# Convolution taps of two channels per TensorE product, flat tables, and masks as seven products, in an S4 + MLP kernel

## The chip, the core and the metric

The kernel runs on one core of a Trainium2 chip. The core has five instruction streams that meet only at semaphores: TensorE (PE, with its weight loads shown apart as PEld), VectorE (DVE), ScalarE (ACT), GpSimd (POOL) and SyncE (SP), which here only issues DMAs. Each stream executes its instructions in the order in which the program lists them. The metric is the device time of one execution in microseconds (us); lower is better.

## The reference, cut to what matters

One sequence of 2048 positions with 512 channels goes through a state-space convolution (S4) and an MLP, each with a residual.

```python
dt = exp(log_dt)[:, None];  logdA = dt * (A_re + 1j*A_im);  dB = dt * (B_re + 1j*B_im)
l = arange(L).astype(bfloat16)                        # positions, rounded to bf16
P = exp(logdA[:, :, None] * l)                        # 512 x 128 x 2048
K = einsum("dn,dnl,dn->dl", C, P, dB).real            # 512 channels x 2048 taps
y = causal_convolution(K, layernorm(x)) + layernorm(x) * Dskip       # by FFT of length 4096
h = x + y
out = h + (gelu(layernorm(layernorm(h)) @ w1 + b1) @ w2 + b2)        # 512 -> 1376 -> 512
```

Since `l` is rounded to bf16, the taps K[d, l] are needed only at positions of the form a + 8b. The exponential of a sum is a product of exponentials, so K at a + 8b is, per channel d, the real part of a sum over the 128 states n of A[n, a] * B[n, b]: a small matrix product with n as the contracted dimension.

## The kernel before, in words

The 128 partitions of the big tables hold the 128 states n. Channels are split into four chunks of 128 (`CW`), c = 0..3, and the chunks into two pairs, q = 0 (c = 0, 1) and q = 1 (c = 2, 3). The program is one recorded list of operations. `Sched.add` records each with its engines, a planned cost and its dependences; the list `ORDER` (L166), found beforehand by a search and written out as numbers, fixes the order in which they are emitted, and with it the order on each engine (a negative number takes the second engine that an operation allows). `Sched.run` goes through `ORDER` once with a planned time, only to choose PSUM slots and to put in filler products (`fill`, L1378), and emits. A flag `hv` marks operations that the planner holds to lock DVE and POOL against each other.

Stages, with the lines of the profile:

1. **Setup.** Small inputs are loaded and transposed (L712, L746). `th` holds dt * A_re (L726, L571, sign turned at L559). `bexps` (L732) writes the magnitudes of the table B by 16 exponentials of 1024 columns; `aexps` (L941, L945, L949, L952) writes those of the table A. BatchNorm statistics of x are L871. POOL makes constants.
2. **Chains** (`chain`, L960). The phases of the tables are gathered in PSUM by products with small weights (L986), read out by ACT as sines and cosines into the buffers `SC` (L988, two of 1024 columns for each group of 4 rows, three buffers in turn), and multiplied into the magnitudes by DVE: B, for each half of the channels four groups of a sine and a cosine product on both sides of a centre row and one change of sign (L1007, L1008, L1006), and A, five groups with two products each (L1007 and L1008 for the first half, L993 and L994 for the second). The centre rows of B are set by POOL (L1313, L1314, L1337, L1338). In this stage POOL also makes the masked weights `W`, 7 x 4 small products of `valW` with a column of `msk` (L561 under `PTS`; the order gives 24 to POOL and 4 to DVE), and `BD` (L1329) and `DD`.
3. **Taps.** For q = 0, `kgen` (L1015) makes for each channel two products (real and imaginary) with 20 columns of A as weights and 33 columns of B as data (L1030, L1031), four channels at a time side by side in four column tiles of 32; both tables hold channels innermost, so neighbouring elements of a product's weights and of its data lie 256 bytes apart. For q = 1, `kgen4` (L1046) makes two products for four channels together, with 128 columns as weights (4 channels x 32 rows, 20 of them used, the pad rows zeroed by L1301 and by a DMA of 768 KB) and 132 columns as data (L1061, L1062); of the 4 x 4 blocks of the result the diagonal is used. Results go from PSUM to `Kg` by `evac` (L513 when ACT takes it, L515 when DVE does).
4. **Spectra.** `kspec` (L1095) maps taps to a first DFT stage with `W`, `kstage` turns the result through DRAM (`AK_d`) and `fstage` (L912) does the second DFT stage. `xspec` (L893, L912) does the same to the input, from `unorm` (L881).
5. **Inverse** (L1135 on DVE, L1145 on PE, turned by transposing DMAs L1151), `tail` (L1214 and following) and the MLP (`mlp`, L1268 to L1292).

```python
o = pst(p)[32 * g:32 * g + NA, 512 * nb:512 * nb + NB * n].rearrange("p (k i) -> p k i", i=n)[:, :, i]
pe.matmul(o, lhsT=Ar.ap()[:, :, d], rhs=Br.ap()[:, :, d], start=True, stop=False, tile_position=(0, 32 * g))
pe.matmul(o, lhsT=Ai.ap()[:, :, d], rhs=Bi.ap()[:, :, d], start=False, stop=True, tile_position=(0, 32 * g))
```

Of the kernel before, what the change touches and what calls it, by code (L numbers as in the profile page):

```python
# [15 lines left out]
P = 128  # L16
# [11 lines left out]
NB = 33  # L28
# [122 lines left out]
class VS(V):  # L151
# [93 lines left out]
class Sched:  # L245
# [42 lines left out]
    def run(self, nslots):  # L288
# [13 lines left out]
        for code in ORDER:  # L302
# [16 lines left out]
            if e == "POOL" and o.hv:  # L319
                for a, b in hold:  # L320
                    if a <= s < b:
                        s, end = b, b + c
# [62 lines left out]
def kernel(ctx, tc, A_u, A_A_re, A_A_im, A_B_re, A_B_im, A_C_re, A_C_im, A_log_dt, A_Dskip,  # L385
# [53 lines left out]
    Dz = take(bf16, NCH, 32)  # L439
# [34 lines left out]
    Kg = [take(bf16, NB, 2, 32), at(sc0 - 512, bf16, NB, 4, 2, 32)]  # L474
    zlo = take(bf16, NB, 2, 32).lo
    AK0 = take(bf16, 16, 2 * CW).lo
    XB = [at(lo + 16384, bf16, 8, 512) for lo in (E0, BA0)]
    PR = [[at(rest0 + 2048 * n, bf16, 8, CW) for n in range(4)], [take(bf16, 8, CW) for _ in range(2)] + [at(lo + 24576, bf16, 8, CW) for lo in (E0, BA0)]]
    Z = [[at(lo, bf16, P, 16) for lo in q] for q in ((zlo, sc0 + 8192), (EA2.lo + 11264, IA2.lo + 11264))]
    assert pos[0] <= NBYTES, pos[0]  # L480
    EA = [at(E0 + c * ASZ, bf16, NA, CW) for c in range(2)]
    EB = [at(EB0 + c * BSZ, bf16, NB, CW) for c in range(NCH)]
    IA = [at(BA0 + c * ASZ, bf16, NA, CW) for c in range(2)]
    IB = [at(IB0 + c * BSZ, bf16, NB, CW) for c in range(NCH)]
    ALL = slice(None)
# [46 lines left out]
    class Tmp:  # L532
# [3 lines left out]
        def __call__(self, dt, *shape):  # L536
# [883 lines left out]
```

## Time and profile before

| | us |
|---|---|
| median of 3 runs (lowest, highest) | 264.26 (263.89, 266.27) |
| the profiled execution | 262.47 |
| its span, first to last instruction | 260.1 |
| busy in the span: PE / DVE / ACT / POOL | 230.3 / 183.3 / 176.8 / 61.8 |
| setup, up to the first product of the chains on DVE | 47.45 |
| chains, to the end of the last of them on DVE | 47.45 to 90.6 |
| taps of q = 1, spectra, start of inverse and MLP | 90.7 to 165 |
| MLP with the rest of the inverse | 165 to 256.5 |

How to read it: a row of a timeline gives start and duration in us, engine, line, operation, what is written from what with its size, how many instructions were merged, and in brackets what the engine waited for. A row of the groups gives the busy time in us, the mean duration of one in ns, and idle time just before. Durations of neighbouring instructions overlap on one engine (they are pipelined), so what an instruction costs in a stream is the distance from start to start. PE busy counts such overlapping records and says little of how full PE is. The granted TensorE clock was 0.999 of full speed over the span.

### The profile page before, as it was taken

To read this page: it belongs to the slowest core of one execution; us is meant where nothing else is said; L and a number is where in the kernel's file an instruction comes from. 1 tells how busy PE (TensorE), PEld (TensorE's weight loads), DVE (VectorE), ACT (ScalarE), POOL (GpSimd) and SP (SyncE) were. 2 spreads that over 40 slices of the span, in tenths; PEclk is the share of its full clock that TensorE was granted. 3 is DMA by queue.
4 is the path that set the end of the run, shared out by engine and by line. 5 is a ranking of instruction groups with operands and counts; after the bars stand their busy time and mean duration, and the time that the engine had idled before them with its cause. 6 is when DMAs were issued, how large, how long until landed. Compare 5 with 4: busy or idle time off the path is not lost.

```text
span 260.1 us, 7656 instructions
## 1 busy us (share of the span) xinstructions
PE 230.3 (89%) x3236; PEld 133.7 (51%) x3249; DVE 183.3 (70%) x368; ACT 176.8 (68%) x214; POOL 61.8 (24%) x234
## 2 busy tenths in 40 slices
PE   7215997888997999989999998899999999999994
PEld 3102673454876586444467765555553434444452
DVE  3999997999999964679899778974615676222021
ACT  2679989999977977578989956966514701762700
POOL 9930871699996000000000000000000000000000
PEclk9999999999999999999999999999999999999999
DMA  6940012000001247729835985560771040214202
GB/s 161 211 108 2 4 38 28 3 4 3 3 5 57 72 164 222 249 93 283 279 112 88 143 161 176 97 170 3 117 131 36 0 93 20 61 28 96 69 15 66
DMA packets 40371, 23.88 MB, mean 92 GB/s; under 512 B 25649, under 2 KB 37778, under 8 KB 40338
## 3 DMA queue, kind: packets, MB, share of 16 engines
q1 hardware_dynamic: 39746, 22.95, 36.8%
q10 hardware_dynamic: 592, 0.46, 0.8%
q8 instruction: 25, 0.41, 0.6%
q14 instruction: 8, 0.07, 0.1%
HBM read 10.03 MB, written 6.29 MB: 63 GB/s over the span
## 4 chain that ended last, share of the span: by engine, by line
PE 57%; DVE 25%; ACT 11%; issue 5%; POOL 0%; DVEq 0%; ACTq 0%; POOLq 0%
PE ps L1268 15%; PE ps L1290 15%; PE ps L1145 8%; PE ps L893 5%; ACT ar L988 4%; ACT ar L513 4%; DVE ar L871 4%; PE ps L912 4%; DVE ar L1007 3%; DVE ar L576 3%; DVE ar L571 2%; PE ps L1095 2%; PE ps L1061 2%; DVE ar L1008 2%; DVE ar L559 2%
## 5 line engine op out<-in xcount | busy, mean ns | idle before, releaser
L513 ACT CAST ar<-ps 128x1024 bf16<-128x1024 f32 (+3 forms) x72 | 65.2, 970 | 19.3 <-PE ps L1145 6.9
L1270 ACT ACTIVATE ar<-ps,ar 128x512 bf16<-128x512 f32 (+1 forms) x44 | 28.2, 686 | 36.7 <-PE ps L1268 36.6
L561 POOL TENSOR_SCALAR ar<-ar 128x128 bf16<-128x128 bf16 (+6 forms) x44 | 39.6, 921 | 7.6 <-ACT ar L583 7.3
L1290 PE MATMUL ps<-ar 128*128 128x512 bf16 (+3 forms) x180 | 39.1, 367 | 0.4
L1268 PE MATMUL ps<-ar 128*128 128x512 bf16 (+1 forms) x176 | 39.3, 379 | 0.0
L515 DVE CAST ar<-ps 128x1024 bf16<-128x1024 f32 (+2 forms) x28 | 30.6, 1113 | 11.9 <-ACT ar L513 4.0
L988 ACT ACTIVATE ar<-ps 128x1024 bf16<-128x1024 int16 x36 | 35.1, 1032 | 5.1 <-DVE ar L1007 1.6
L1135 DVE TENSOR_TENSOR ar<-ar 128x1024 bf16<-128x1024 bf16 x48 | 30.7, 687 | 10.3 <-PE ps L1145 9.9
L1292 DVE TENSOR_TENSOR ar<-ps,ar 128x512 bf16<-128x512 f32 (+1 forms) x17 | 11.1, 660 | 37.7 <-PE ps L1290 35.0
L1290 PEld LDWEIGHTS <-ar 128*128 128x128 bf16 (+1 forms) x187 | 17.9, 98 | 20.0 <-issue 0.8
L1268 PEld LDWEIGHTS <-ar 128*128 128x128 bf16 (+1 forms) x176 | 17.3, 100 | 20.5 <-issue 0.8
L986 PE MATMUL ps<-ar 128*32 128x256 f16 x560 | 21.4, 275 | 5.0 <-ACT ar L988 3.1
L1145 PEld LDWEIGHTS <-ar 64*128 64x128 bf16 x768 | 21.6, 94 | 5.4 <-issue 3.0
L1145 PE MATMUL ps<-ar 64*128 64x128 bf16 x768 | 23.9, 217 | 0.3 <-ACT ar L513 0.3
L986 PEld LDWEIGHTS <-ar 128*32 128x32 f16 x560 | 14.3, 97 | 12.5 <-issue 12.2
L912 PE MATMUL ps<-ar 128*64 128x512 bf16 (+1 forms) x160 | 17.7, 342 | 1.2 <-DMA ar<-AK_d 0.6
L732 ACT ACTIVATE ar<-ar 128x1024 bf16<-128x1024 f32 x16 | 15.6, 1041 | 3.2 <-DVE ar L559 3.2
L893 PE MATMUL ps<-ar 128*32 128x512 bf16 x256 | 16.0, 381 | 0.3 <-ACT ar L513 0.3
L576 DVE SCALAR_TENSOR_TENSOR ar<-ar 128x4 f32<-128x4 f32 (+5 forms) x44 | 14.2, 327 | 2.5 <-ACT ar L583 1.4
L583 ACT ACTIVATE ar<-ar 128x512 f32<-128x512 f32 (+8 forms) x18 | 11.9, 681 | 4.9 <-DMA ar<-in_A_log_dt_dram 1.8
L1008 DVE TENSOR_TENSOR ar<-ar 128x1024 bf16<-128x1024 bf16 x21 | 14.6, 719 | 0.0
L1007 DVE TENSOR_TENSOR ar<-ar 128x1024 bf16<-128x1024 bf16 x21 | 14.5, 716 | 0.1
(99 smaller groups left out, 318.6 us busy)
## 6 DMA issues: line engine op xcount, KB each, us to landing
ar<-AK_d SPq DMA_DIRECT2D x8, 512.0 KB, 5.6
ar<-in_A_u_dram SPq DMA_DIRECT2D x4, 512.0 KB, 9.2
AK_d<-ar SPq DMA_DIRECT2D x2, 1024.0 KB, 4.6
AK_d<-ar SPq DMA_DIRECT2D x4, 512.0 KB, 4.0
out_dram<-ar SPq DMA_DIRECT2D x30, 64.0 KB, 2.0
ar<-in_B_w_dram SPq DMA_DIRECT2D x4, 344.0 KB, 6.0
ar<-in_B_w_dram SPq DMA_DIRECT2D x2, 640.0 KB, 6.6
ar<-ar SPq DMA_DIRECT2D x1, 768.0 KB, 5.4
```

Of the source, the lines that this page charges most:

```text
L513: act.copy(out_fn(), in_fn())
L515: dve.tensor_copy(out_fn(), in_fn())
L561: en.tensor_scalar(a, b, f(s1), f(s2), op0, op1)
L893: pe.matmul(pst(p)[32 * cg:32 * cg + 32, 512 * z:512 * z + 512], lhsT=BD.ap()[:, 32 * f + 2 - 2 * jl:32 * f + 34 - 2 * jl], rhs=un[2 * (2 ...
L912: pe.matmul(pst(p)[64 * h:64 * h + 64, w * (k + r):w * (k + r) + w], lhsT=T.ap()[:, f, r, :], rhs=v[f:f + 1].ap()[:, 0, :], start=True, st ...
L986: pe.matmul(pst(p)[32 * g:32 * g + 32, 256 * j:256 * j + 256], lhsT=W2[DELTAS.index(d)].ap(), rhs=S2[g].ap()[:, ch0:ch0 + 256], start=Fals ...
L988: add("ACT", c_act(1024), lambda e, p=p, sc=sc, cs=cs: act.activation(swo(sc[cs]) if hf and kind == "B" else sc[cs].ap().rearrange("p a b ...
L1135: dve.tensor_tensor(o, a, b_[:, :, ::-1, :] if sw else b_, ALU.mult)
L1145: pe.matmul(pst(p)[:, 512 * h + 128 * k:512 * h + 128 * k + 128], lhsT=q.ap()[rows, 2 * k + r, :], rhs=TP[w].ap()[rows, f0 // 2 + k, :], s ...
L1268: pe.matmul(pst(p)[:fs, 512 * z:512 * z + 512], lhsT=w1s[dc].ap()[:, fc * P:fc * P + fs], rhs=ybuf.ap().rearrange("p (t c) k -> p c t k", ...
L1270: add("ACT", c_act(512, 1), lambda e, p=p, z=z, fc=fc, fs=fs: act.activation(hT.ap()[:fs, fc, :], pst(p)[:fs, 512 * z:512 * z + 512], ACT. ...
L1290: pe.matmul(pst(p)[:, 512 * z + c0:512 * z + c1], lhsT=hT.ap()[:fs, fc, 128 * t:128 * t + 128], rhs=w2s[fc].ap()[:fs, c0:c1], start=(fc == ...
```

## The change

It does the following; numbers of lines are those of the kernel before unless said otherwise.

- One `kgen(q)` takes the place of `kgen` and `kgen4`. For each of the 64 channel places d of a pair's half, and for two such halves s side by side in two column tiles of 64, a product has 52 columns of A as weights: 20 rows of one chunk, 12 rows of zeros, 20 rows of the other chunk of the pair, 64 bytes from element to element. Its data are 72 columns of B: 2 chunks x 9 groups x 4 neighbouring rows, in runs of 4 elements. Of the 2 x 2 blocks (chunk by chunk) the diagonal is used. Each pair has 256 products (before: 512 for q = 0, 128 for q = 1) and 5 evacuations of 1008 or 864 columns (before: 4 of 726 or 330 columns for q = 0, 12 of 792 or 264 for q = 1).
- A lies as 4 x 52 x 32 per pair, B as 9 groups x 1024 (128 channel places x 2 chunks x 4 rows) per pair. All of `EB`, `IB`, and both pairs of `EA`, `IA` are laid out this way; the four gaps of zeros are filled by four memsets (`gap`), which takes the place of L1301 and of the DMA of 768 KB. The centre of B is a group of its own.
- The DVE products of the B chains take 1024 elements in one run, those of the A chains 2 x 4 runs of 128. ACT does the reordering when it writes sines and cosines (L988) and magnitudes.
- `Kg` has 37 instead of 33 rows, one of them a copy; `kspec` reads runs of 64 instead of 32 channels.
- The 28 small mask products become 7 of 512 elements each, `valW` times an expanded mask `mskx` (one copy of 896 elements). The order gives all of these to POOL.
- `th` is made by two products of 256 columns (before: two of 256 and two of 128) and turned in sign by two operations; one 512-column product goes from POOL to DVE. The table `TPc` is kept once instead of twice; one ACT operation of 1024 columns becomes two of 512.
- Many buffers move; `ORDER` is new throughout; the planner adds 0.3 us to a POOL operation that it holds to be waiting for DVE. The order has 27 filler products instead of 42, and moves the ACT operation of 2048 columns that makes the table `T` from behind the chains into them.

```diff
-    IA2 = at(BA0 + 2 * ASZ + NCH * BSZ, bf16, 2, 4, 32, 32)
-    EA2 = at(IA2.hi, bf16, 2, 4, 32, 32)
+    EA, IA = ([at(lo, bf16, 4, 52, 32) for lo in q] for q in ((E0, EA2), (BA0, IA2)))
+    EB, IB = ([at(lo + q * BPR, bf16, 9, 1024) for q in range(2)] for lo in (EB0, IB0))
...
+    def gap(v):
+        rows = [at(v.lo + 3328 * m + 1280, bf16, 12, 32) for m in range(4)]
+        o = lambda: raw_ap(v.lo + 1280, (1664, 4), (1, 384)).bitcast(f32)
+        add(("DVE", "POOL"), (0.5, 0.5), lambda e: (dve if e == "DVE" else gp).memset(o(), 0.0), w=rows, hv=1)
...
-                add("DVE", c_dve(1024, 2), lambda e, lo=lo, rv=rv, Sx=Sx, e0=e0, i0=i0, q=q: dve.tensor_tensor(ent(i0, q, lo, 4, rv), ent(e0, q, lo, 4, rv), Sx(), ALU.mult), r=rE + [sc[0]], w=rI)
+                add("DVE", c_dve(1024, 2), lambda e, E_=E_, I_=I_, sc=sc: dve.tensor_tensor(I_.ap(), E_.ap(), flat(sc[0]), ALU.mult), r=[E_, sc[0]], w=[I_])
...
-    def kgen(c, pr):
-    def kgen4(c, pr):
+    def kgen(q, pr):
+        kg = Kg[q]
+        xs = [lambda x, v=v: v.ap().rearrange("p g (x c j) -> p x c g j", c=2, j=4)[:, x] for v in (EB[q], IB[q])]
+        i0 = 0
+        for n, h in enumerate((7, 7, 6, 6, 6)):
+            p = Ps()
             for b in range(2):
+                def fn(e, p=p, i0=i0, h=h, b=b):
                     for jj in range(h):
+                        d = i0 + h * b + jj
+                        for n, (A_, x) in enumerate(zip((EA[q], IA[q]), xs)):
+                            for s in range(2):
+                                m, i = 2 * s + (d >> 5), d & 31
+                                o = pst(p)[64 * s:64 * s + 52, 512 * b + 72 * jj:512 * b + 72 * jj + 72].rearrange("p (c g j) -> p c g j", c=2, j=4)
+                                pe.matmul(o, lhsT=A_.ap()[:, m, :, i], rhs=x(32 * m + i), start=(n == 0), stop=(n == 1), tile_position=(0, 64 * s))
...
     for v in range(7):
-        for g in range(4):
-            PTS(W[v], valW, msk[4 * v + g:4 * v + g + 1], n=128, oap=lambda v=v, g=g: W[v].ap()[:, :, 32 * g:32 * g + 32], pr=2.05)
+        TT(W[v], valW, mskx[v], ALU.mult, n=512, mode=2, oap=lambda v=v: W[v].ap().rearrange("p t (g c) -> p t g c", g=4), aap=lambda: valW.ap().unsqueeze(2).to_broadcast([P, 4, 4, 32]),
+           bap=lambda v=v: mskx[v].ap().unsqueeze(1).to_broadcast([P, 4, 4, 32]), pr=2.05, eng="POOL")
...
-    dma("SP", lambda: pads(IA2), lambda: pads(EA2), 786432, [EA2], [IA2], pr=3.45)
+    gap(IA[0])
+    gap(IA[1])
```

More of the change, by code (lines that the diff above doesn't have):

```diff
@@ L438 @@
     DD = take(bf16, 2, 16, 4)
-    Dz = take(bf16, NCH, 32)
+    Dz = take(bf16, 2, 64)
     b1_bf = take(bf16, 11)
@@ L700 @@
     S.pr = 0.2
-    dtb = tE(bf16, 512)
     AC(dtb, ldt, ACT.Exp, tbl=True)
@@ L714, in tr @@
         return p, (lambda: nat(pst(p, bf16)[:, 0:512]))
-    th = tL(f32, 5, 256)
-    thn = lambda: th.ap().rearrange("p h d -> p (h d)").rearrange("p (a q) -> p a q", q=256)[:, 2:5:2, :]
+    th = tL(f32, 4, 256)
     p, pa = tr("are")
-    TT(th[2], p, dtb, ALU.mult, n=256, psum=True, oap=by4(th[2], 0, 256), aap=lambda pa=pa: pa()[:, 0:64], bap=by4(dtb, 0, 256))
-    def th3(e, p=p):
-        for c in range(2):
-            o = th[3].ap().rearrange("p (c e d g) -> p c e d g", c=2, e=8, d=4)[:, c]
-            x = pst(p, bf16)[:, 0:512].rearrange("p (d c g e) -> p c e d g", d=4, c=4, g=4)[:, 2 + c]
-            y = dtb.ap().rearrange("p (c g e d) -> p c e d g", c=4, g=4, e=8)[:, 2 + c]
-            dve.tensor_tensor(o, x, y, ALU.mult)
@@ L727 @@
-    add("DVE", c_dve(256, 1, True), th3, r=[p, dtb], w=[th[3]], hv=0)
-    TT(th[4], p, dtb, ALU.mult, n=256, psum=True, oap=by4(th[4], 0, 256), aap=lambda pa=pa: pa()[:, 64:128], bap=by4(dtb, 256, 512), pr=0.42)
-    TS(th[0:2], th[2:4], -1.0, None, ALU.mult, n=512, pr=0.35)
+    thv = lambda h: th[h].ap().rearrange("p (q d c) -> p c q d", d=4, c=2)
+    thn = lambda: th[0:2].ap().rearrange("p h (x c) -> p h c x", c=2)
+    nat3 = lambda v: v.ap().rearrange("p (h c x) -> p h c x", h=2, c=2)
+    for hf in range(2):
+        TT(th[hf], p, dtb, ALU.mult, n=256, psum=True, oap=lambda hf=hf: thv(hf), aap=lambda hf=hf, p=p: pst(p, bf16)[:, 0:512].rearrange("p (d h c q) -> p h c q d", d=4, h=2, c=2)[:, hf],
+           bap=lambda hf=hf: dtb.ap().rearrange("p (h c q d) -> p h c q d", h=2, c=2, d=4)[:, hf], pr=0.2 + 0.22 * hf)
+        TS(th[2 + hf], th[hf], -1.0, None, ALU.mult, n=256, pr=0.35)
@@ L730, in bexps @@
     def bexps(pr):
         for e0 in range(1, 17):
-            add("ACT", c_act(1024) + 0.03, lambda e, e0=e0: act.activation(multi(EB0, BSZ, bf16, NCH, NB, CW)[:, :, 16 - e0:17 + e0:2 * e0, :].rearrange("p c k d -> p k c d"), th[0:4].ap().rearrange("p (k h) (c d) -> p k (h c) d", k=2, c=2), ACT.Exp, scale=float(8 * e0)),
-                r=[th[0:4], TBL], w=[EB[c][16 + z * e0] for z in (1, -1) for c in range(NCH)], pr=pr + 0.01 * e0)
+            g, j = (e0 - 1) // 4, (e0 - 1) % 4
+            o = lambda g=g, j=j: raw_ap(EB[0].lo + 2048 * g + 2 * j, (5 * 1024, 2), (9 * 1024, 2), (4, 256))
@@ L735 @@
+            add("ACT", c_act(1024) + 0.03, lambda e, o=o, e0=e0: act.activation(o(), th[0:4].ap().rearrange("p (k h) x -> p k h x", k=2), ACT.Exp, scale=float(8 * e0)),
+                r=[th[0:4], TBL], w=[EB[q][g + z] for z in (0, 5) for q in range(2)], pr=pr + 0.01 * e0)
     bexps(1.0)
@@ L819 @@
     add("DVE", c_dve(928), lambda e: dve.tensor_reduce(msk.ap(), R.ap(), mybir.AxisListType.X, ALU.add), r=[R], w=[msk], pr=1.55)
-    wi = ct(i32, 4, 16)
+    mskx = ct(bf16, 7, 4, 32)
+    mx = lambda e: (dve.tensor_copy if e == "DVE" else gp.tensor_copy)(mskx.ap().rearrange("p v g c -> p (v g) c"), msk[0:28].ap().unsqueeze(2).to_broadcast([P, 28, 32]))
+    add(("POOL", "DVE"), (0.9, 1.0), mx, r=[msk], w=[mskx], pr=1.55, hv=1)
+    wi = tE(i32, 4, 16)
     for tl in range(4):
@@ L872 @@
     stats(st, nw, 16, 1.0, EPS, 1.25, ln=True)
-    UN = [[X0s[j] for j in range(7)] + [at(zlo + 1024 * b, bf16, 512)] for b in range(2)]
+    UN = [X0s[j] for j in range(8)]
     def unorm(b, pr):
-        un = UN[b]
+        un = UN
         for j in range(8):
@@ L987, in chain @@
                 add("PE", 0.55 + (0 if gn else 0.45 if kind == "B" else 1.3), fn, r=[W2, S2, Wm, cst] + ([HLo, I16] if kind == "A" and gn == 0 else []), w=[p], new=[p] if gn == 0 else [])
-                add("ACT", c_act(1024), lambda e, p=p, sc=sc, cs=cs: act.activation(swo(sc[cs]) if hf and kind == "B" else sc[cs].ap().rearrange("p a b -> p (a b)"), swi(p) if hf and kind == "B" else pst(p, i16).rearrange("p (n two) -> p n two", two=2)[:, :, 0], ACT.Sin, scale=SINSC), r=[p, TBL], w=[sc[cs]])
+                add("ACT", c_act(1024), lambda e, p=p, sc=sc, cs=cs: act.activation(sco(sc[cs]), sci(p), ACT.Sin, scale=SINSC), r=[p, TBL], w=[sc[cs]])
@@ L989, in chain @@
             mark = [("cg", kind, hf, gn)]
-            if dm:
-                E_, I_ = (lambda b0=b0: dmaj(EA2, b0)), (lambda b0=b0: dmaj(IA2, b0))
-                f_ = [lambda sc=sc, z=z: sc[z].ap().rearrange("p a (x i) -> p x a i", x=8) for z in range(2)]
-                add("DVE", c_dve(1024, 2), lambda e, E_=E_, I_=I_, f_=f_: dve.tensor_tensor(I_(), E_(), f_[0](), ALU.mult), r=[EA2, sc[0]], w=[IA2])
-                add("DVE", c_dve(1024, 2), lambda e, E_=E_, f_=f_: dve.tensor_tensor(E_(), E_(), f_[1](), ALU.mult), r=[EA2, sc[1]], w=[EA2] + mark)
-                continue
@@ new lines, in chain @@
+            if kind == "A":
+                rE, rI = aregs(EA[hf], b0), aregs(IA[hf], b0)
+                oE, oI = (lambda v=v, b0=b0: arows(v[hf], b0, (1, 128)) for v in (EA, IA))
+                f = [lambda z=z, sc=sc: flat(sc[z]).rearrange("p (c m x) -> p c m x", m=4, c=2) for z in range(2)]
+                add("DVE", c_dve(1024, 2), lambda e, oE=oE, oI=oI, f=f: dve.tensor_tensor(oI(), oE(), f[0](), ALU.mult), r=rE + [sc[0]], w=rI)
+                add("DVE", c_dve(1024, 2), lambda e, oE=oE, f=f: dve.tensor_tensor(oE(), oE(), f[1](), ALU.mult), r=rE + [sc[1]], w=rE + mark)
+                continue
@@ L1046, in kgen4 @@
-    def kgen4(c, pr):
-        Ar, Br, Ai, Bi = EA2[c - 2], EB[c], IA2[c - 2], IB[c]
-        kg = Kg[c // 2]
-        for j0 in range(0, 32, 6):
-            S.pr = pr + 0.01 * (j0 // 6)
-            p = Ps()
-            n = min(6, 32 - j0)
-            h = (n + 1) // 2
+                add("DVE", c_dve(1024, 2), lambda e, E_=E_, I_=I_, sc=sc: dve.tensor_tensor(I_.ap(), E_.ap(), flat(sc[0]), ALU.mult), r=[E_, sc[0]], w=[I_])
+                add("DVE", c_dve(1024, 2), lambda e, E_=E_, sc=sc: dve.tensor_tensor(E_.ap(), E_.ap(), flat(sc[1]), ALU.mult), r=[E_, sc[1]], w=[E_] + mark)
@@ L1164 @@
     XBc = [Two([VS(v, c) for v in XB]) for c in range(NCH)]
-    y2T = [at(lo, bf16, 16, P) for lo in (Kg[0].lo + 11264, W.lo, T.lo)]
+    y2T = [at(lo, bf16, 16, P) for lo in (BA0 + 28672, W.lo, T.lo)]
     hT = at(Kg[0].lo, bf16, NFC, 512)
-    w1s = [at(EA2.lo + 2752 * c, bf16, F) for c in range(4)]
-    w2s = [at(IA2.lo + 1024 * fc, bf16, 512) for fc in range(11)]
+    w1s = [at(IA2 + 2752 * c, bf16, F) for c in range(4)]
+    w2s = [at(IA2 + 11008 + 1024 * fc, bf16, 512) for fc in range(11)]
     ots = [at(sc0 + 8192 + 1024 * n, bf16, 512) for n in range(8)]
@@ L1299 @@
     S.pr = 8
-    pads = lambda v: v.ap().rearrange("p c g a i -> p (c g) a i")[:, :, NA:32, :]
-    add("DVE", 1.0, lambda e: dve.memset(pads(EA2), 0.0), w=[EA2], pr=0)
     load_small()
@@ L1335 @@
         PTS(DD, valD, mD[g:g + 1], n=32, oap=lambda g=g: DD.ap()[:, :, :, g], pr=4.5)
-    for c in range(2, 4):
-        add("POOL", 0.2, lambda e, c=c: gp.memset(EB[c][16].ap(), 1.0), w=[EB[c][16]], pr=1.7, hv=1)
-        add("POOL", 0.2, lambda e, c=c: gp.memset(IB[c][16].ap(), 0.0), w=[IB[c][16]], pr=1.71 + 0.01 * (c // 2))
-    dma("SP", lambda: pads(IA2), lambda: pads(EA2), 786432, [EA2], [IA2], pr=3.45)
+    center(1)
+    gap(IA[0])
+    gap(IA[1])
     unorm(0, 3.4)
@@ L1344 @@
     for q in range(2):
-        for c in (2 * q, 2 * q + 1):
-            (kgen if q == 0 else kgen4)(c, 5.1 + 4 * c)
+        kgen(q, 5.1 + 8 * q)
         for n, bs in enumerate(KB[q]):
```

191 lines of the change are left out of this document (80 added, 111 removed), and 71 rows, old and new, of the table ORDER.

## The prediction

> **What bounds the kernel now.** I read the busy shares first, then the busy time of each engine by stretch (start:end, length, then busy us with counts), then timelines of the chains and of the taps.
>
> ```profile
> PE 230.3 (89%) x3236; PEld 133.7 (51%) x3249; DVE 183.3 (70%) x368; ACT 176.8 (68%) x214; POOL 61.8 (24%) x234
> PE 57%; DVE 25%; ACT 11%; issue 5%; POOL 0%; DVEq 0%; ACTq 0%; POOLq 0%
> ```
> ```profile
> 47.00:90.70 43.70, 38.49 (x1105) 26.66 (x1106) 43.35 (x77) 39.07 (x47) 34.66 (x34) 1.00 0.07 21
> 90.70:165.00 74.30, 71.67 (x1253) 44.40 (x1257) 57.89 (x94) 59.90 (x65) 0.52 (x1) 1.00 0.64 173
> 165.00:256.50 91.50, 90.57 (x667) 45.37 (x672) 40.81 (x103) 41.24 (x61) 0.00 (x0) 1.00 0.34 69
> ```
>
> There are three regimes. In the chains DVE is busy 43.35 of 43.70 us and ACT 39.07: DVE sets the end. From 90.7 to 165 PE leads, but DVE (78%) and ACT (81%) are close behind and their evacuations hold PE up. From 165 on PE is full. The change touches the first two.
>
> ```profile
> L513 ACT CAST ar<-ps 128x1024 bf16<-128x1024 f32 x60 | 57.7, 1028 | 16.1 <-PE ps L1145 6.9 <-PE ps L893 3.4 <-PE ps L1095 2.9
> L1135 DVE TENSOR_TENSOR ar<-ar 128x1024 bf16<-128x1024 bf16 x48 | 30.7, 687 | 10.3 <-PE ps L1145 9.9 <-ACT ar L513 0.4
> L561 POOL TENSOR_SCALAR ar<-ar 128x128 bf16<-128x128 bf16 x24 | 26.4, 1113 | 7.3 <-ACT ar L583 7.3
> L515 DVE CAST ar<-ps 128x1024 bf16<-128x1024 f32 x20 | 24.0, 1221 | 6.9 <-PE ps L912 3.7 <-ACT ar L513 2.1 <-PE ps L893 0.3
> L1008 DVE TENSOR_TENSOR ar<-ar 128x1024 bf16<-128x1024 bf16 x21 | 14.6, 719 | 0.0
> L515 DVE CAST ar<-ps 128x792 bf16<-128x792 f32 x6 | 5.8, 981 | 2.5 <-ACT ar L513 1.9 <-PE ps L1062 0.6
> L513 ACT CAST ar<-ps 128x792 bf16<-128x792 f32 x4 | 3.3, 843 | 0.8 <-PE ps L1062 0.8
> L571 POOL TENSOR_TENSOR ar<-ar 128x512 f32<-128x512 f32 x2 | 2.5, 1272 | 0.7 <-DVE ar L576 0.7
> ```
>
> These are the prices: the evacuations of taps (792 columns), a chain product with and without long runs (L1135, L1008), a small mask product, and the nearest thing to a new one (POOL, 512 columns).
>
> ```profile
> 25.73 2.15 POOL L571 TENSOR_TENSOR ar<-ar 128x928 f32<-128x928 f32 x1 [10.17 <-DVE ar L559]
> ```
> ```profile
> 26.16 2.27 DVE L576 SCALAR_TENSOR_TENSOR ar<-ar 128x512 f32<-128x512 f32 x1
> ```
>
> A DVE operation that takes 0.69 us elsewhere (21.18) took 2.27 when it fell into a POOL product of 928 columns: it lost 1.58 and ended 0.55 after POOL did.
>
> ```profile
> 66.62 0.27 PE L1031 MATMUL ps<-ar 128*20 128x33 bf16 x4
> 66.68 0.28 PE L1030 MATMUL ps<-ar 128*20 128x33 bf16 x4
> 66.75 0.27 PE L1031 MATMUL ps<-ar 128*20 128x33 bf16 x4
> ```
> ```profile
> 91.40 0.22 PE L1061 MATMUL ps<-ar 128*128 128x132 bf16 x1
> 91.46 0.23 PE L1062 MATMUL ps<-ar 128*128 128x132 bf16 x1
> 91.52 0.22 PE L1061 MATMUL ps<-ar 128*128 128x132 bf16 x1
> ```
>
> Four old products of q = 0 start together each 0.069 us (17.2 ns apiece; 88 between 66.55 and 68.04); those of q = 1 follow each other by 0.062 us.
>
> **The change part by part,** against the profiled execution (262.47; span 260.1 and 2.4 around it). The median is 1.8 above it, which I add at the end.
>
> *Setup (to 47.45).* L726 and L571 (0.64 + 0.42 + 0.41) become two products of 0.41: -0.65. The sign change at 6.67 (1.87, beside POOL's constants) becomes two of half the size, in the same company: -0.6, between -1.2 and 0. One product of 512 (0.69) and two small operations (0.35) come over from POOL. Together -0.2, between -1.5 and +1. L1301 (1.34 at 1.13) stood before DVE's wait until 5.66 and gives nothing; nor does the DMA of 768 KB (issued at 82.04, the next SP transfer at 90.58).
>
> *Chain products.* 52 products and 8 sign changes stay. Undisturbed they follow by 0.60 (83.08, 83.68, 84.28) in pieces of 128 or 512. L1135, all in one run, has 687 ns against 716 and 719: at best 42 x 0.03 = 1.3 less, and I take 0.
>
> *Masks.* Out: four on DVE at 0.298 = 1.2, and 24 on POOL. Eleven chain products from 55.38 to 62.55 took 7.17 instead of 6.6, beside six mask products: 0.1 apiece, 2.4. In: seven of 512. By the 928-column product one costs DVE 1.58 x 512/928 = 0.87; by the 128-column one at 64.42 (two chain products in 1.49 against 1.28) 0.2 x 4 = 0.8. Seven are 6.0. The copy of 896 costs 0.7 (beside the 1024-column L561 on POOL two sign changes took 1.63 against 0.85). That is 6.7 if each falls on a working DVE and 0 if all fall into waits; the stretch has few waits, but the new masks stand among A products, where ACT gives 1.9 us of work for each 1.2 of DVE. I take two thirds, 4.5. Net +0.9, between -3.6 and +3.1.
>
> *Taps of q = 0.* PE falls from 512 x 17.2 ns = 8.8 to about 4.9 under a full DVE: 0. The new evacuations are 1008, 864 and (spectra) 1024 columns on DVE at 1.19 ns, 3.4, against two at 86.28 (2.35); two fewer unorm at 0.36; the copy and the sum +0.2: net +0.5. ACT gets 1.9 for T, 0.4 for evacuations and 0.2 for the split table: 41.6 of 43.7, hidden under DVE. If ACT were late, at most +2.
>
> The chains thus end at +1.2.
>
> *Taps of q = 1.* Out: 128 x 62 ns = 7.9. In: 256. L1030's tile takes 69 ns for 33 single elements, 2.08 each; L1061 takes 62 ns for 33 runs of 4, 1.88 each. Eighteen runs of 4 are 34 to 37 ns in a tile, and two tiles run side by side as four did: 17 to 19 ns. At 19: 4.9, so -3.0. The upper end is the second rival.
>
> *Evacuations of q = 1.* Out: 6 x 0.981 + 2 x 0.434 on DVE, 4 x 0.843 on ACT: 10.1. In: 1.2 + 2 x 1.03 on DVE, 1.01 + 0.88 on ACT: 5.2. T leaves this stretch (1.9), unorm and the copy add 0.9. That is 5.9 less on two engines, 3.0 each. Both are about 80% busy, so I take half: -1.5, between -3 and 0.
>
> *Spectra.* 48 products of 256 at 0.03 move ahead and 16 of 512 at 0.055 come behind: -0.5. Fillers stand only in gaps: 0. From 165 on nothing changes.
>
> Sum: 1.2 - 3.0 - 1.5 - 0.5 = -3.8, so 258.7 for an execution like the profiled one, and 260.5 against the median. The new order can misplace a few us either way; no row prices that.
>
> [...] The row at 26.16 shows DVE held until POOL's product was through. [...] L1030 costs 17.2 ns with 20 weight columns. [...]
>
> **The rivals.**
>
> 1. *POOL's masks hold DVE for all their time.* 7 x 1.27 + 0.9 = 9.8 instead of 4.5: +5.3, 265.8. For it: 26.16, and DVE's 0.35 us of idle time in the stretch. Against it: ACT is nearly as full, and what ACT delays can be lost twice. It decides from about 5 us on. Chance 0.20.
> 2. *Weights, not data, pace the new products.* 17.2 ns for 20 columns is 0.86 a column; 52 are 44.7 ns, 256 of them 11.4 us behind the chains, more than the old 7.9, and the sum is +2.7: 267.0, slower than before. For it: the weights stay 64 bytes apart, and L1061's loads take 145 ns where contiguous ones (L1145) take 94. Against it: L1061 loads 128 such columns within 62 ns. It decides from 30 ns a product on. Chance 0.15.
> 3. *The savings behind the chains are hidden* by the way through DRAM (taps, write, read, second DFT stage) that q = 1 has to go anyway; only +1.2 and -0.5 are left: 265.0, no change. For it: PE waits on evacuations there. Against it: PE busy 71.67 of 74.30. Chance 0.12.
> 4. *The masks fall into ACT's time and the evacuations pay in full:* 4.5 + 1.5 less than forecast, 254.5. Chance 0.15.
>
> **How the numbers follow.** The forecast (0.38) has its own range of 257 to 264 for setup, order and half-hidden terms. 1% is about what a measurement of this kernel tells from no change: the bounds are 261.6 and 266.9. Faster: 0.27 of the forecast, all of rival 4, 0.02 of rival 3: 0.44. Slower: 0.09 of the first rival, 0.10 of the second, 0.05 of third and forecast: 0.24. The rest, 0.32, is the same. The range 254 to 268.5 leaves out about 0.06 below (rival 4 with a lucky order) and 0.12 above (rivals 1 and 2 together or with a poor order).
>
> **What would show it.** New tap products two at a time each 0.035 to 0.040 us (0.09 would be rival 2); seven POOL products near 1.3 us, with DVE products of 1.5 to 2 us beside them in all (rival 1) or half of the cases; last A product at 91 to 93; five evacuations of taps of 1 to 1.2 us for q = 1; from there to the end some 5 us less than 166. I am wrong if the stretch behind the chains is not shorter, or if the chains end past 95.

## The result and the profile after

The changed kernel takes 290.84 us (median of 4 runs, 290.42 to 292.86) against 264.07 of the kernel before beside it: a ratio of 1.102, 95% interval 1.093 to 1.112. It is 10% slower, on the other side from the forecast of 260.5 and above its range. Executions of one kernel fall into a faster and a slower state, and the ratios below compare the faster alone, with runs of the kernel before taken beside them (medians of 260.3 to 264.1 us). The profiled execution took 290.42, its span 288.3 (before 262.47 and 260.1). Where the 28.2 us of span went, by the start of the first and the end of the last product of the chains on DVE:

| us of the span | before | after | forecast against before |
|---|---|---|---|
| up to the first chain product | 47.45 | 62.49 | -0.2 |
| chains | 43.2 | 54.2 | +1.4 |
| behind the chains | 169.5 | 171.7 | -5.0 |

All three stretches are longer. The page of the changed kernel, busy shares and chain of waits:

```profile
PE 238.3 (83%) x3106; PEld 139.0 (48%) x3106; DVE 186.8 (65%) x366; ACT 194.4 (67%) x207; POOL 48.9 (17%) x214
...
PE 60%; ACT 22%; issue 7%; POOL 5%; DVE 4%; DMA 1%; DVEq 0%; ACTq 0%; POOLq 0%
```

Three signs stand here at once. ACT is busy 17.6 us longer, with fewer instructions (207 against 214), and has doubled its share of the chain that ended last, from 11 to 22%. POOL does less work and yet has 5% of that chain, where it had none. PE is busy 8 us longer with 130 products fewer: some of its products have become dearer.

The groups of the changed kernel say which lines (busy us, mean ns of one | idle time before them); the second fence has the rows of the kernel before for the same exponentials and for the sines:

```profile
L521 ACT CAST ar<-ps 128x1024 bf16<-128x1024 f32 (+3 forms) x67 | 62.8, 985 | 31.7 <-PE ps L1023 13.0
L523 DVE CAST ar<-ps 128x1024 bf16<-128x1024 f32 (+2 forms) x27 | 32.2, 1203 | 21.5 <-PE ps L1023 13.3
L745 ACT ACTIVATE ar<-ar 128x1024 bf16<-128x1024 f32 x16 | 38.2, 2541 | 1.2 <-DVE ar L567 1.2
L988 ACT ACTIVATE ar<-ps 128x1024 bf16<-128x1024 int16 x36 | 34.8, 1045 | 5.2 <-DVE ar L1002 2.0
L1023 PE MATMUL ps<-ar 128*52 128x72 bf16 x512 | 25.4, 266 | 4.7 <-DVE ar L996 4.7
L1023 PEld LDWEIGHTS <-ar 128*52 128x52 bf16 x512 | 24.5, 187 | 7.2 <-issue 7.0
```
```profile
L732 ACT ACTIVATE ar<-ar 128x1024 bf16<-128x1024 f32 x16 | 15.6, 1041 | 3.2 <-DVE ar L559 3.2
L988 ACT ACTIVATE ar<-ps 128x1024 bf16<-128x1024 int16 x36 | 35.1, 1032 | 5.1 <-DVE ar L1007 1.6 <-DVE ar L1008 1.6 <-PE ps L986 1.4
```

The 16 exponentials of B (L732 before, L745 after) take 2541 ns each instead of 1041: 22.6 us more of ACT, for the same number of elements. The sines (L988), which also write a new order, cost what they did (1045 against 1032). And ACT and DVE now wait 26 us in all for the tap products L1023.

The busy time of each engine by stretch of the changed kernel (start:end, length, then PE, PEld, DVE, ACT, POOL with counts, granted clock, DMA share, GB/s):

```profile
62.49:80.00 17.51, 13.59 (x278) 7.84 (x271) 17.51 (x33) 17.38 (x22) 4.39 (x2) 1.00 0.01 2
80.00:94.00 14.00, 7.43 (x145) 5.38 (x147) 13.59 (x13) 7.38 (x9) 13.91 (x12) 0.78 0.01 2
94.00:116.65 22.65, 22.11 (x470) 16.83 (x466) 17.65 (x31) 16.80 (x18) 3.77 (x6) 0.99 0.01 2
116.65:131.90 15.25, 15.25 (x319) 13.39 (x312) 5.86 (x8) 4.87 (x6) 0.00 (x0) 1.00 0.43 141
131.90:288.30 156.40, 147.78 (x1715) 77.80 (x1713) 95.59 (x192) 90.84 (x112) 0.00 (x0) 0.99 0.46 110
```

In the second stretch DVE is busy 13.59 of 14.00 us with 13 records; in the first, at the same fullness, 33 records take 17.51. Its instructions last twice as long there, and POOL is busy all the time. In the third and fourth PE is the full engine, DVE and ACT wait. The timelines of DVE and of POOL in the second stretch:

```profile
80.61 1.29 DVE L1002 TENSOR_TENSOR ar<-ar 128x1024 bf16<-128x1024 bf16 x1
81.82 1.64 DVE L995 TENSOR_TENSOR ar<-ar 128x1024 bf16<-128x1024 bf16 x1
83.38 1.37 DVE L1001 TENSOR_SCALAR ar<-ar 128x1024 bf16<-128x1024 bf16 x1
84.67 1.64 DVE L996 TENSOR_TENSOR ar<-ar 128x1024 bf16<-128x1024 bf16 x1
...
93.60 0.68 DVE L1003 TENSOR_TENSOR ar<-ar 128x1024 bf16<-128x1024 bf16 x1
```
```profile
76.29 5.07 POOL L834 CAST ar<-ar 128x896 bf16<-128x896 f32 x1
81.44 4.32 POOL L579 TENSOR_TENSOR ar<-ar 128x512 bf16<-128x512 bf16 x3
...
87.69 5.84 POOL L579 TENSOR_TENSOR ar<-ar 128x512 bf16<-128x512 bf16 x4
```

Beside POOL's masks DVE's operations follow each other by 1.2 to 1.6 us, one for each mask; before and after them chain products follow by 0.60. From 80.61 to 93.60 DVE did seven chain products and three smaller operations, about 5.3 us of work (7 x 0.60 and 3 x 0.36), in 13.0. So some 7.7 us were lost. ACT gave no cover for it: it had 7.38 us of work in these 14.00, and DVE never waited for it.

The tap products follow each other by 46.3 ns (112 of them start within 5.14 us for q = 1; 56 within 2.52 for q = 0), against 19 ns in the forecast and 44.7 in its second rival.

### The profile page after: what moved, and what is told of

Read it like the earlier page. It is cut to its first block, busy times and chain, and to the rows that moved or that the text cites. A ratio compares the mean times of both kernels' runs of the same rounds, so it can differ in the third digit from the quotient of the medians.

```text
span 288.3 us, 7352 instructions
## 1 busy us (share of the span) xinstructions
PE 238.3 (83%) x3106; PEld 139.0 (48%) x3106; DVE 186.8 (65%) x366; ACT 194.4 (67%) x207; POOL 48.9 (17%) x214
## 4 chain that ended last, share of the span: by engine, by line
PE 60%; ACT 22%; issue 7%; POOL 5%; DVE 4%; DMA 1%; DVEq 0%; ACTq 0%; POOLq 0%
PE ps L1234 13%; PE ps L1256 13%; ACT ar L745 12%; PE ps L1023 9%; PE ps L1111 7%; PE ps L909 5%; ACT ar L521 4%; PE ps L928 4%; PE ps L1061 3%; ACT ar L951 2%; POOL ar L834 2%; PE ps L986 2%; PE ps L1180 2%; POOL ar L579 1%; DMA ar<-in_A_log_dt_dram 1%
## 5 line engine op out<-in xcount | busy, mean ns | idle before, releaser
L521 ACT CAST ar<-ps 128x1024 bf16<-128x1024 f32 (+3 forms) x67 | 62.8, 985 | 31.7 <-PE ps L1023 13.0
L523 DVE CAST ar<-ps 128x1024 bf16<-128x1024 f32 (+2 forms) x27 | 32.2, 1203 | 21.5 <-PE ps L1023 13.3
L1256 PE MATMUL ps<-ar 128*128 128x512 bf16 (+2 forms) x187 | 39.6, 367 | 0.0
L745 ACT ACTIVATE ar<-ar 128x1024 bf16<-128x1024 f32 x16 | 38.2, 2541 | 1.2 <-DVE ar L567 1.2
L988 ACT ACTIVATE ar<-ps 128x1024 bf16<-128x1024 int16 x36 | 34.8, 1045 | 5.2 <-DVE ar L1002 2.0
L1101 DVE TENSOR_TENSOR ar<-ar 128x1024 bf16<-128x1024 bf16 x48 | 30.6, 686 | 8.2 <-PE ps L1111 7.3
L1023 PE MATMUL ps<-ar 128*52 128x72 bf16 x512 | 25.4, 266 | 4.7 <-DVE ar L996 4.7
L1023 PEld LDWEIGHTS <-ar 128*52 128x52 bf16 x512 | 24.5, 187 | 7.2 <-issue 7.0
L948 PE MATMUL ps<-ar 128*128 128x256 f16 x80 | 13.2, 329 | 6.6 <-ACT ar L951 6.6
L944 PE MATMUL ps<-ar 128*128 128x512 f16 x24 | 8.2, 467 | 11.3 <-DVE ar L567 10.1
L1346 PE MATMUL ps<-ar 128*128 128x512 bf16 x27 | 7.4, 389 | 10.4 <-DMA ar<-in_A_u_dram 9.9
```

The source lines that it names most:

```text
L521: act.copy(out_fn(), in_fn())
L523: dve.tensor_copy(out_fn(), in_fn())
L745: add("ACT", c_act(1024) + 0.03, lambda e, o=o, e0=e0: act.activation(o(), th[0:4].ap().rearrange("p (k h) x -> p k h x", k=2), ACT.Exp, s ...
L988: add("ACT", c_act(1024), lambda e, p=p, sc=sc, cs=cs: act.activation(sco(sc[cs]), sci(p), ACT.Sin, scale=SINSC), r=[p, TBL], w=[sc[cs]])
L1023: pe.matmul(o, lhsT=A_.ap()[:, m, :, i], rhs=x(32 * m + i), start=(n == 0), stop=(n == 1), tile_position=(0, 64 * s))
L1101: dve.tensor_tensor(o, a, b_[:, :, ::-1, :] if sw else b_, ALU.mult)
```

## The experiments

Three suspects, then: exponentials of B, masks on POOL, weights of the taps. Each has a rival reading. In the diffs, lines with a minus are the changed kernel's; most are shortened, some to the order of the elements alone (x channel place, c chunk, j tap position, g group).

**One edit each, from the changed kernel.** The first, with runs for the exponentials:

```diff
-            o = lambda g=g, j=j: raw_ap(EB[0].lo + 2048 * g + 2 * j, (5 * 1024, 2), (9 * 1024, 2), (4, 256))
+            o = lambda g=g, j=j: raw_ap(EB[0].lo + 2048 * g + 512 * j, (5 * 1024, 2), (9 * 1024, 2), (1, 256))
```

> The changed kernel with one edit: the 16 exponentials of B (L745) write four runs of 256 instead of 1,024 single elements 8 bytes apart. The values land in another order than the products assume, so the output is not the reference's; every count, size and order is kept. Theory (the write step is what costs: 2541 ns against 1041 before, and these 16 hold ACT and with it the first chain product back from 47.45 to 62.49): L745 about 1.04 us, first chain product near 48, time 14 to 16 us below the changed kernel's 290.8, so 275 to 277. Rival (the exponentials are slow through how they read th, or through what runs beside them, or the chains wait for something else in the new order): L745 stays above 2 us, or falls while the first chain product stays near 62; time 286 to 291.

Measured: 276.71 us, ratio 1.060 (1.044 to 1.076); L745 at 1.04 us; the first chain product at 43.87, earlier even than the kernel before. The write step is the cause of the late start, and the rival falls. Of the 18.6 us by which the chains start earlier, 12.5 reach the end of the span: the chains take 56.6 us instead of 54.2, and what follows 175.3 instead of 171.7. The granted clock was lower for longer here than in the changed kernel (0.86, 0.90 and 0.61 in the stretches from 57 to 118 us; these lines are in the last section); whether that or the order took the rest was not tried.

The second keeps runs for ACT in another way, with the tap position outermost, and thereby asks what the data of the tap products cost:

```diff
-  EB, IB: "p g (x c j) -> p x c g j"      # 18 runs of 4 for one product
+  EB, IB: "p g (j x c) -> p x c g j"      # 72 single elements; exponentials as above, sines in the same order
```

> The changed kernel with the four tap positions of a chunk outermost (j x c in place of x c j) in the exponentials, the sines and the products of B, so ACT writes runs of 256, and the tap products read their data as 72 single elements 512 bytes apart in j instead of 18 runs of 4. The same function is computed. Theory A (weights, 52 columns 64 bytes apart, set the 49 to 50 ns of a tap product): tap products stay at 49 to 52 ns, the time is that of the kernel with runs in the exponentials, 275 to 277. Theory B (data set it, at 1.9 to 2.1 ns for every run or single element and two products side by side): 72 x 2 / 2 = 70 to 75 ns, 512 x 22 ns = 11 us more PE time, of which the half of q=1 lies on the path: 281 to 288. My own forecast term of 19 ns came from B's rule with 18 runs.

Measured: 298.45 us, ratio 1.143 (1.130 to 1.157). Tap products 83 ns apart (112 within 9.18 us). Theory B's mechanism, at 1.15 ns for each element, but dearer than its 70 to 75 ns and 288 us: data can be what paces these products. It does not say that they were before the edit.

The third moves the masks:

```diff
-    add(("POOL", "DVE"), (0.9, 1.0), mx, r=[msk], w=[mskx], pr=1.55, hv=1)
+    add(("DVE", "POOL"), (1.0, 0.9), mx, r=[msk], w=[mskx], pr=1.55, hv=1)
...
-           bap=lambda v=v: mskx[v].ap().unsqueeze(1).to_broadcast([P, 4, 4, 32]), pr=2.05, eng="POOL")
+           bap=lambda v=v: mskx[v].ap().unsqueeze(1).to_broadcast([P, 4, 4, 32]), pr=2.05)
```

> The changed kernel with the copy that spreads the mask values (L834) and the seven mask products moved from POOL to DVE, at the same places in the order. Theory (POOL's 5.07 + 7 x 1.48 us hold DVE's products beside them for as long as POOL works): the eight operations cost DVE about 0.5 to 0.9 + 7 x 0.35 = 3.2 us, every chain product is back at 0.60 to 0.72, the chain stretch (62.5 to 116.6) is 5 to 9 us shorter, time 282 to 286. Rival (the slow products beside POOL were in ACT's or PE's time anyway, as the forecast's two thirds say in part): products are fast again but the last one ends within 3 us of 116.6, time 288 to 291.

Measured: 286.46 us, ratio 1.098 (1.085 to 1.110). The chain products are back at 0.68 (median; the longest of the 52 took 0.88); the chains take 50.4 us instead of 54.2, 3.8 less, between the two expectations. Here the runs alone don't separate it well from the changed kernel (1.102); the clean test is below.

The fourth reads the weights in a run:

```diff
-  pe.matmul(o, lhsT=A_.ap()[:, m, :, i], ...)
+  pe.matmul(o, lhsT=A_.ap()[:, m].rearrange("p a i -> p (a i)")[:, 52 * i:52 * i + 52], ...)
```

> The changed kernel with the weights of every tap product read as 52 neighbouring columns instead of 52 columns 64 bytes apart (other columns than the reference's, so the output is not its; the count, the size and the data of the products are kept). Theory A (the weights' step sets 49 to 50 ns): 20 to 30 ns a product, PE about 10 to 13 us less in taps, q=1's taps 5 to 7 us shorter and q=0's hold the chains less: time 281 to 285. Theory B (data or the number of products sets it): products stay at 45 to 50 ns, time 289 to 291.

Measured: 279.75 us, ratio 1.072 (1.059 to 1.085), a little below theory A. Products 21.2 ns apart (112 within 2.35 us); the chains take 50.4 us and the rest 164.1, 5.4 less than before. The two groups of this kernel, to be set beside the 266 and 187 ns above:

```profile
L1023 PE MATMUL ps<-ar 128*52 128x72 bf16 x512 | 12.9, 214 | 3.8 <-DVE ar L996 3.8
L1023 PEld LDWEIGHTS <-ar 128*52 128x52 bf16 x512 | 11.7, 114 | 6.5 <-DVE ar L996 3.9 <-issue 2.6
```

With the same data, the same count and the same size, only the weight step makes 46 of 21 ns. The weight loads are 73 ns shorter each.

**All three at once, and each taken back alone.** If there were a fourth cause, it had to show here.

> The changed kernel with all three edits of before at once: exponentials of B written in runs of 256, mask copy and products on DVE, tap weights read as 52 neighbouring columns (exponentials and weights not at the places that the reference needs). Theory (these three are all that went against the forecast, and they add up): first chain product 43.9, chain stretch 54.2 - 3.8 - 3.7 = 46.6, the rest 164 as in the kernel with neighbouring weights: span near 255, time 256 to 258, some 2% below the kernel before; that would be the forecast's -3.8. Rival (they overlap: with an early start alone the chain stretch grew from 54.2 to 56.6, so something else, ACT's sines or the order, holds the chains): 261 to 265, not faster than before.

Measured: 257.19 us, ratio 0.979 (0.975 to 0.984), as the theory had it. The stretches of this kernel:

```profile
43.76:57.00 13.24, 10.29 (x215) 6.01 (x204) 13.04 (x26) 12.85 (x17) 0.12 (x1) 1.00 0.01 3
57.00:69.00 12.00, 9.18 (x175) 5.42 (x177) 12.00 (x24) 10.46 (x12) 7.42 (x9) 1.00 0.00 1
69.00:89.37 20.37, 19.20 (x559) 13.61 (x562) 19.30 (x36) 18.92 (x20) 0.74 (x1) 1.00 0.01 4
89.37:97.00 7.63, 7.63 (x284) 6.02 (x282) 5.67 (x9) 3.86 (x4) 0.00 (x0) 1.00 0.52 169
97.00:255.10 158.10, 148.28 (x1705) 79.33 (x1713) 95.58 (x192) 91.05 (x112) 0.00 (x0) 0.98 0.45 114
```

DVE is full throughout the chains again, with 24 records in 12.00 us where the changed kernel had 13 in 14.00, and behind them the taps of q = 1 are through after 7.6 us instead of 15.3. The chains take 45.6 us, what follows 165.8.

Now one cost at a time is put back into it.

> The kernel with all three edits (257.2) with one taken back: mask copy and products on POOL, as in the changed kernel (exponentials and weights still not where the reference needs them). The first rival's price by itself: it said 7 x 1.27 + 0.9 = 9.8 us of POOL time reach the end, the forecast 4.5 of them and 2 for the eight operations on DVE are what the comparison gives back. Rival 1: 257.2 + 9.8 - 3 (DVE's own cost of the eight) = 264; the forecast's two thirds: 257.2 + 4.5 - 3 = 259; in the changed kernel itself the edit gave 4 us.

Measured: 263.04 us (median of six runs, 260.6 to 263.96), ratio 1.002 (0.998 to 1.006): 0.023 of 263, that is 6.0 us more than with the masks on DVE. The profiled execution was the fastest, its span 3.6 above; its chains take 50.6 us instead of 45.6. What follows takes 164.1 instead of 165.8, at a granted clock of 1.00; the kernel with all three edits had 0.91 from 149 to 169 us. So in the chains, where the masks stand, they cost 5.0 us, between the forecast's 259 and the first rival's 264; by the runs it is nearly the rival's. On POOL the copy took 1.42 us and the seven products 10.6; on DVE these rows, in the kernel with all three edits, stand against them:

```profile
L579 DVE TENSOR_TENSOR ar<-ar 128x512 bf16<-128x512 bf16 x7 | 2.8, 417 | 0.0
L834 DVE CAST ar<-ar 128x896 bf16<-128x896 f32 x1 | 0.6, 621 | 0.0
```

DVE does in 3.4 us itself what holds it for 8 to 9 when POOL does it (3.4 and the 5.0 or 6.0).

> The kernel with all three edits (257.2) with one taken back: tap weights 64 bytes apart, as in the changed kernel (exponentials still in another order than the reference needs). The second rival's price by itself: 256 x (46.3 - 21.2) = 6.4 us for the products of q=1, which nothing covers, and as much for q=0, which I had taken as hidden under a full DVE. If q=0 is hidden: 257.2 + 6.4 = 263.6; if it holds the chains, too: up to 270. In the changed kernel the edit gave 11 us, of which 3.7 in the chains.

Measured: 269.79 us, ratio 1.024 (1.014 to 1.035): 11.8 us, the upper end. The last chain product ends at 94.40 instead of 89.37, so 5.0 of it come from q = 0 in the chains, and what follows takes 171.9 instead of 165.8: 6.2 from q = 1.

> The kernel with all three edits (257.2) with one taken back: B's exponentials written one element at a time 8 bytes apart, as in the changed kernel (tap weights still at other columns than the reference needs). It is the price by itself of a term that my forecast does not have. If all of it reaches the end: the first chain product moves from 43.8 to 62.4, so 257.2 + 18.6 = 276. If the chains make some of it good (ACT has then nothing left but sines and is ahead of DVE): 14 to 16, 271 to 273. In the changed kernel the edit gave 12.5 us of the profiled span.

Measured: 275.98 us, ratio 1.050 (1.043 to 1.056): 18.5 us. The first chain product is at 62.55, the last one ends at 108.45, 45.9 after it: the whole delay goes through to the end.

The three prices, 18.5, 6.0 and 11.8, sum to 36.3; from 0.979 to 1.102 are 32.5. The 3.8 between them can be overlap, or no more than what such differences can tell (the intervals of the ratios are 0.01 wide or so, 2 to 3 us each). Either way no fourth cause is needed.

**How the costs depend on the step.** Both strides were made 4 bytes in one kernel:

```diff
-  exponentials: raw_ap(EB[0].lo + 2048 * g + 2 * j, ..., (4, 256))
+  exponentials: raw_ap(EB[0].lo + 2048 * g + 1024 * (j // 2) + 2 * (j % 2), ..., (2, 256))
-  weights: lhsT=A_.ap()[:, m, :, i]                                          # 64 bytes apart
+  weights: lhsT=A_.ap()[:, m].rearrange("p a i -> p (a i)")[:, 48 * i:48 * i + 104:2]    # 4 bytes apart
```

> The changed kernel with both strides halved or less: B's exponentials written with a step of 4 bytes instead of 8, tap weights with a step of 4 bytes instead of 64 (values land and are read at other places, so the output is not the reference's). Theory A (any step beside contiguous costs about the full price): exponentials 2.3 to 2.5 us, tap products 42 to 47 ns, time 285 to 291. Theory B (the price falls with the step): exponentials 1.4 to 2.0 us, tap products 21 to 35 ns, time 265 to 282.

Measured in a single run: 265.76 us, beside 263.05 of the kernel before. Both go by theory B, to its lower ends and a little below:

```profile
L745 ACT ACTIVATE ar<-ar 128x1024 bf16<-128x1024 f32 x16 | 20.1, 1333 | 1.1 <-DVE ar L567 1.1
L1023 PEld LDWEIGHTS <-ar 128*52 128x52 bf16 x512 | 12.2, 119 | 7.3 <-DVE ar L996 4.0 <-issue 3.3
```

An exponential costs 1.33 us at 4 bytes, 2.54 at 8; with weights 4 bytes apart the products come as fast as with contiguous ones and the same data (120 within 2.52 us, 21 ns). As the data pace them there, weights at 4 bytes may still cost something that this kernel doesn't show.

**The plan without its costs.** Two kernels went half of the way. First, tap position outermost, data as 36 runs of 2, masks on DVE:

```diff
-  EB, IB: "p g (x c j) -> p x c g j";  PSUM of a product: (c g j)
+  EB, IB: "p g (j x c) -> p x g j c";  PSUM of a product: (g j c), turned by the evacuation
```

> The same function as the reference: tap position outermost in B (so ACT writes runs of 256, as in the second kernel), but the tap products take their data as 36 runs of 2 and leave the swap to the evacuations; masks on DVE. Theory (product = the longer of weights, 46 ns, and data, at most 83/72 = 1.15 ns for each run, 41 ns): products at 46 to 50 ns, time 271 to 274 (276.7 of the kernel with contiguous exponentials, less 4). Rival (weights and data add: 46 - 21 + 41 = 66 ns): 512 x 20 = 10 us more PE time, 277 to 283.

Measured: 270.54 us, ratio 1.028 (1.023 to 1.033); products 46 ns apart (112 within 5.11 us; single groups of them from 45 to 50): weights and 36 runs don't add, the longer of the two counts. Then the same with A's 52 rows innermost:

```diff
-  raw_ap(v.lo + 64 * a0, (1024, 2), (1664, 4), ...)      # A of (4, 52, 32): runs of 32 and 128
+  raw_ap(v.lo + 2 * a0, (32, 2), (52, 128), (1, 4))      # A of (4, 32, 52): runs of 4, 104 bytes apart
```

> The same function as the reference: as the kernel with runs of 2 and masks on DVE, and the A table with its 52 rows innermost, so that the tap weights are contiguous; ACT then writes A's exponentials, and DVE reads and writes A's products, in runs of 4 elements 104 bytes apart. Theory A (runs of 4 cost ACT and DVE little): ACT's exponentials of A near 1.1, DVE's A products near 0.7, tap products 40 to 42 ns (data), time 262 to 266. Theory B (runs of 4 are near single elements): ACT up to 2.5 us each (10 x 1.4 = 14 us), DVE's 20 A products 1.1 to 1.2 us each (+10 us): 272 to 285.

Measured: 266.54 us, ratio 1.014 (1.010 to 1.019), just above theory A's range. Its rows are theory A's: ACT's exponentials of A stay at 1.01 us and DVE's products of A at 0.686 although both now go in runs of 4; the tap products, 41 ns apart, are paced by their 36 runs. What was left was an order of B that gives ACT pairs and TensorE longer runs (the input `th` and the sines are put in the same order, and some buffers move by 2 KB):

```diff
-  raw_ap(EB[0].lo + 2048 * g + 2 * j, (5 * 1024, 2), (9 * 1024, 2), (4, 256))      # (x c j): single elements
+  raw_ap(EB[0].lo + 2048 * g + 4 * j, (5 * 1024, 4), (8, 128), (1, 2))             # (x j c): pairs, 16 bytes apart
-  EB, IB: "p g (x c j) -> p x c g j"
+  EB, IB: "p g (x y) -> p x g y", y=8                                              # 9 runs of 8 for one product
```

> The same function as the reference. As the kernel with A's rows innermost and masks on DVE, but B ordered channel, tap position, half (x j c): ACT writes B's exponentials in runs of 2 elements 16 bytes apart, and a tap product reads its data as 9 runs of 8. Theory A (what costs ACT is the single element; pairs are near free, as the runs of 4 in A were): exponentials 1.0 to 1.35 us, tap products 20 to 22 ns with contiguous weights, time 256 to 260, 1 to 2.5% below the kernel before: that would be the change's plan without its three costs, computing what the reference does. Theory B (cost goes by the number of separate places written, and they lie 16 bytes apart): exponentials 1.9 to 2.6 us, chains begin 8 to 15 us later than 43, time 266 to 275.

Measured: 256.45 us (4 runs, 255.46 to 258.03), ratio 0.976 (0.969 to 0.982): faster than both kernels, with the reference's whole function. Its rows:

```profile
L745 ACT ACTIVATE ar<-ar 128x1024 bf16<-128x1024 f32 x16 | 17.0, 1123 | 1.2 <-DVE ar L567 1.2
...
L1023 PE MATMUL ps<-ar 128*52 128x72 bf16 x512 | 9.9, 199 | 0.2 <-DVE ar L996 0.2
L1023 PEld LDWEIGHTS <-ar 128*52 128x52 bf16 x512 | 8.9, 107 | 4.2 <-issue 4.0 <-DVE ar L897 0.2
```

The exponentials pay 0.08 us for their pairs, and the tap products come 16.3 ns apart (112 within 1.81 us), less than the 20 to 22 expected here and the 19 of the forecast.

## Why the prediction was wrong, step by step

**Setup: the step that failed most.** The forecast's "Together -0.2" leaves out that the exponentials of B write single elements 8 bytes apart. The section on the change says that ACT does the reordering when it writes; the sum had no term for it, not even a bound, because the trace of before had no such write. It costs 18.5 us, more than half of the 32.5. The forecast could still have said that no row prices such a write, and that these 16 operations stand ahead of all the chains. The rest of the setup was misjudged in the other direction: without this cost the first chain product starts at 43.8, 3.7 before the old kernel's, where the forecast had 0.2. Which part of the change gives that was not tried.

**Taps: the term "19 ns a product" was mis-sized, and the second rival was right.** The reading of the rows in runs and elements was right for the data: 18 runs of 4 do take 21 ns once the weights are contiguous, and 9 runs take 16. But the longer of data and weights counts (46 ns in the kernel with 36 runs of data and weights 64 bytes apart, 41 there with the weights in a run), and for weights the rival's 0.86 ns a column, taken from L1030, gives 44.7, measured 46.3; two products took 0.093 us, the sign that the prediction named for this rival. My argument against it was L1061, which loads 128 such columns within 62 ns. Here 52 columns 64 bytes apart took 46 all the same, so that row did not carry over to this shape; why it is so much faster there no run has shown. Nor do the columns alone set the pace: the same 52 in a run came 21.2 ns apart with the same data, and 16.3 in the last kernel. The step of the weights counts.

**Taps of q = 0 under a full DVE: 0.** Wrong once a product takes 46 ns: 5.0 of the 11.8 us were lost in the chains, where evacuations of these taps stand in DVE's queue and wait for PE.

**Masks: two thirds of the price.** The first rival was nearer: 3.8 us in the span (in the changed kernel) to 6.0 by the runs against DVE doing them itself, and 3.4 that DVE needs for that, so 7 to 9 of the rival's 9.8, where the forecast had 4.5. Its sign came too: five chain products of 1.55 to 1.65 us beside the seven masks. ACT's waits gave no cover. The price of one mask was near (1.48 us a product, in the prediction 1.27). DVE started seven operations beside the seven masks (81.82 to 92.43), one for each.

**Behind the chains: right where the weights don't spoil it.** Forecast 5.0 less than 169.5; measured 5.4 less with contiguous weights alone, 3.7 with all three edits, 2.2 more in the changed kernel. The terms in it for evacuations and spectra were not measured apart.

**The sum.** The forecast's -3.8 is about what the plan gives without the three costs: -5.5 us by the ratio of 0.979, the setup's 3.7 and the masks on DVE included. That is luck in part: by stretches of the span it is -3.7, +2.4 and -3.7 against the forecast's -0.2, +1.4 and -5.0. Its statement of what would make it wrong (stretch behind the chains not shorter, or chains ending past 95) came true on both counts: 171.7, and 116.65.

## What to carry to other kernels

Here a new layout put the cost on the engine that writes it (ACT's exponentials, 2.54 us instead of 1.04), so give every instruction whose access pattern changes a term of its own, the writers' as well as the readers', and where no row prices the new pattern, a bound that lets the sign flip. Ask of each table for the shortest run in each of its uses: here an order existed that gave ACT pairs, DVE runs of 4 or more and TensorE contiguous weights and runs of 8, and of the orders tried that compute the reference's function only that one, with the masks on DVE, made two channels for one product pay. Work moved in bigger pieces to POOL beside a full DVE was not moved away here: it was cheaper for DVE to do it (3.4 us against 8 to 9).

## What the runs showed of the hardware that was not expected

- ACT's writes of bf16: 1.04 us for 1024 columns in runs of 256, 1.12 in pairs 16 bytes apart, 1.01 in runs of 4 that lie 104 bytes apart (the exponentials of A, which read PSUM), 1.33 as single elements 4 bytes apart, 2.54 at 8 bytes. Two elements in every 16 bytes thus cost 0.08 us more than runs of 256 when they lie together, and 1.5 us more when they lie 8 bytes apart.
- Data of tap products, with two column tiles side by side: 72 columns in 9 runs 16.3 ns, in 18 runs 21, in 36 runs 41, in 72 single elements 83 (there with weights 64 bytes apart, at a granted clock of 0.67 over the stretch from 114 to 140 us). From 18 runs on that is 1.14 to 1.17 ns a run.
- In the kernel with runs for the exponentials alone the granted clock was down to 0.61 in the taps of q = 1 (below are its lines by stretch, the clock third from the end). The tap products kept their pace: 120 of them start within 5.44 us from 108.27 on, where the clock was 0.50, so 45.7 ns apart, against 46.3 at 1.00 in the changed kernel. So the pace with weights 64 bytes apart was the same at half the clock. With contiguous weights it was not: in the kernel with that edit alone 56 products from 92.80 on, at 0.50, start within 1.63 us, 29.6 ns apart, against 21.2 at 1.00. Why the clock fell in a stretch with PE full was not tried.

```profile
57.00:75.00 18.00, 9.44 (x169) 5.17 (x170) 18.00 (x18) 11.42 (x12) 17.91 (x16) 0.86 0.00 1
75.00:100.52 25.52, 24.98 (x526) 19.56 (x530) 18.59 (x33) 18.09 (x20) 1.89 (x3) 0.90 0.01 3
100.52:118.00 17.48, 17.48 (x319) 13.76 (x312) 5.84 (x8) 4.88 (x7) 0.00 (x0) 0.61 0.48 155
```

- POOL took longer beside DVE, too: POOL's copy of 896 columns took 5.07 us in the changed kernel, while DVE's products went on at 0.60 until 80.6. In the kernel with the masks put back on POOL it took 1.42, and there the DVE product that started after it (at 58.30) took 1.42 instead of 0.68. What decides which of the two takes longer was not settled.
